# Top-32 attention and a routed MoE on one core: counts compared on GpSimd, and mask and maximum of 16 early tiles applied by TensorE products

## The chip, the cores and the metric

The kernel runs as one program on one core of one Trainium2 chip. A core has five engines that run their own instruction streams in order and meet at semaphores: TensorE (PE, with its weight loads shown as PEld), VectorE (DVE), ScalarE (ACT), GpSimd (POOL) and SyncE (SP, which only issues transfers here). The metric is the device time of the whole program in microseconds, as a median over runs.

## The reference

```python
scores = scale * np.matmul(q, k.transpose(0, 1, 3, 2))      # 8 batches, 8 heads, 576 x 576, head_dim 64
kth = np.partition(scores, -32, axis=-1)[..., -32:-31]
scores = np.where(scores >= kth, scores, -1000000000.0)
attn = np.exp(scores - np.max(scores, axis=-1, keepdims=True))
attn = attn / (np.sum(attn, axis=-1, keepdims=True) + 1e-09)
x = (attn @ v) laid out as 4608 tokens x 512
logits = x @ w_gate + modality_bias[modality_id]            # 8 experts
e_idx = np.argmax(logits, axis=1);  gate_w = softmax(logits) at e_idx
for e in range(8):                                          # every token goes to one expert
    out[e_idx == e] = gate_w[...] * (np.maximum(x[e_idx == e] @ w1[e], 0.0) @ w2[e])
```

## The kernel before

The scores are worked on in 288 tiles of 128 rows by 576 columns; a pair of heads is nine tiles, four pairs are one batch. One loop (L1123) has one pass per tile and works on tiles at different depths of a pipeline: in pass i TensorE computes the scores of tile i+2, VectorE takes the maxima of tile i in six pieces (L396) and merges those of tile i-1 (L407 to L409), ScalarE counts by a Sign with an accumulator how many scores lie above the 24th largest value (L428, tile i-3), GpSimd multiplies scores and signs into `y` (L434, tile i-4), VectorE takes the next eight values out of `y` (L438, tile i-5), and for every third tile it turns the counts of three tiles into the 32nd largest value `kth` (L445 to L447, `pick`): `eq` compares a table of numbers with the counts, `jk` multiplies it with the candidates, a sum leaves the threshold. At the end of pass i VectorE masks tile i-7. The transposes of tile i-9 follow on TensorE (L492), their evacuation on ScalarE (L500), and the products with V for roles 3, 7 and 8 of the nine (L520).

There are two ways to mask. For the tiles from 48 on, and for every third one before, ScalarE takes the exponential of the scores minus the row maximum (L452), and VectorE's `keep` (L458) multiplies it with the mask and sums the row. For the other tiles below 48 ("early", L1012), VectorE's `hide` (L465) writes a penalty of zero or minus 2^100, GpSimd adds it to the scores (L471, `ex<-Ssb,hT`), and ScalarE takes the exponential with the row sum (L477).

The order on VectorE inside a pass is written by a small planner (`arrange`, L949) from a table of durations; the other engines get the instructions as the code emits them. On GpSimd a pass is: the addition L471 for tile i-8, or for a tile masked by `keep` a one-element copy (`gate`, L481) that waits for `keep`; then `y` (L434), in every ninth pass the filling of the block-diagonal queries (L346), then the bound for the count (L421, `n`) and for every third tile the negated maxima (L415, `sm`).

The first batch has to be routed to its experts before the MoE products can start; until then TensorE runs six products with ones in each pass (`keep_warm`, L973), which nobody reads. From then on the MoE work is dealt out to the passes by a budget of TensorE cost per pass. What is left of it runs after the last tile. MoE weights lie in `w1b` and `w2b`, its gathered rows in `xgT` and its hidden layer in `hT`.

Of the kernel before, what the change touches and what calls it, by code (L numbers as in the profile page):

```python
# [35 lines left out]
QL = 2  # L36
KW = 10
FILL = 0
KP = 2
# [17 lines left out]
QO = 0  # L57
# [20 lines left out]
def kernel(  # L78
# [357 lines left out]
    def find(i):  # L436
        t = T[i]
        V.max(t["mg"][:, i % 3, 24:32], t["y"])  # L438

    def pick(i):  # L440

        t = T[i]
        eq, v = (wk.tile([128, 3, 9], FT, name=nm, bufs=1) for nm in ("eq", "jk"))
        n = t["n"][:, 0, :]
        return [lambda: V.tensor_tensor(eq, i9s, n[:, :, None].to_broadcast([128, 3, 9]), op=OP.is_equal),  # L445
                lambda: V.tensor_tensor(v, eq, t["mg"][:, :, 23:32], op=OP.mult),
                lambda: V.tensor_reduce(kth[:, i - 2:i + 1], v, axis=AX.X, op=OP.add)]  # L447
# [19 lines left out]
    def hidden(i):  # L467
# [1022 lines left out]
```

## Time and profile before

| | |
|---|---|
| median of 3 runs | 1193.73 us (1190.71 to 1193.77) |
| the profiled execution's own time | 1191.36 us |
| span of its profile | 1189.7 us |
| busy: PE, DVE, ACT, POOL | 1150.4, 1089.2, 981.5, 670.6 us |
| chain that ended last, by engine | PE 64%, DVE 23%, ACT 6%, issue 2%, DMA 2%, POOL 1% |

The time of the run has 1.7 us around the span. The busy time of an engine counts from the start of a record to its end, and records of neighbours overlap by some tens of nanoseconds on every engine, so what an instruction takes out of a stream is read from its start to the start of the next. The slices of the page show VectorE, TensorE and ScalarE nearly full from the second slice to the 34th (about 30 to 1000 us), and TensorE with VectorE at half from there on, where only MoE work is left.

### The profile page before, as it was taken

How to read it: one execution, taken by the hardware profiler on the slowest of the kernel's cores; microseconds unless marked ns; L12 is line 12 of the kernel's file. 1: busy time of each engine (PE TensorE's matmuls, PEld its weight loads, DVE VectorE, ACT ScalarE, POOL GpSimd, SP SyncE). 2: the span in 40 equal slices, each digit the busy share in tenths (PEclk: the TensorE clock that was granted, in tenths of full speed). 3: DMA queues.
4: the chain of work that ended last, by engine and by line, in shares of the span. 5: the costliest groups of instructions: out<-in, count | busy, mean ns of one | idle time of the engine just before them, and what ended most of it. 6: DMA issues, size and time to landing. Idle time of an engine off the chain costs nothing.

```text
span 1189.7 us, 28032 instructions
## 1 busy us (share of the span) xinstructions
PE 1150.4 (97%) x7902; PEld 904.1 (76%) x7902; DVE 1089.2 (92%) x5474; ACT 981.5 (83%) x2015; POOL 670.6 (56%) x1256
## 2 busy tenths in 40 slices
PE   8889979999999999999999999999999999999998
PEld 6667768777777868777686877778687777589987
DVE  7999999999999999999999899999999999476762
ACT  5999979998889979998999899989999887355653
POOL 6888875555656565566566566557655665221111
PEclk9999999999999999999999999999999999999999
DMA  5663357653677368654785448664765554287750
GB/s 125 161 183 90 89 164 221 191 151 87 169 221 199 86 178 241 170 151 129 199 244 156 129 134 242 168 163 133 204 185 134 173 145 148 71 288 250 245 191 22
DMA packets 204323, 197.09 MB, mean 166 GB/s; under 512 B 104413, under 2 KB 151533, under 8 KB 204160
## 3 DMA queue, kind: packets, MB, share of 16 engines
q1 hardware_dynamic: 196880, 175.92, 53.4%
q0 software_dynamic: 6080, 19.00, 4.4%
q8 instruction: 66, 1.08, 0.4%
q14 instruction: 97, 0.79, 0.2%
q10 hardware_dynamic: 1200, 0.30, 0.1%
HBM read 118.63 MB, written 24.23 MB: 120 GB/s over the span
## 4 chain that ended last, share of the span: by engine, by line
PE 64%; DVE 23%; ACT 6%; issue 2%; DMA 2%; POOL 1%; SPq 0%; POOLq 0%; ACTq 0%; DVEq 0%
PE E L798 11%; PE E L811 11%; PE X L520 10%; PE S L384 8%; PE T L492 7%; DVE cand L396 6%; PE X L1085 5%; PE X L1069 4%; DVE mg L438 4%; DVE P L458 4%; PE E L1069 1%; PE X L318 1%; ACT K L428 1%; ACT Ssb L389 1%; DVE cand L407 1%
## 5 line engine op out<-in xcount | busy, mean ns | idle before, releaser
L396 DVE MAX8 cand<-Ssb 128x8 f32<-128x96 f32 x1728 | 389.5, 245 | 2.1 <-ACT Ssb L389 2.1
L434 POOL TENSOR_TENSOR y<-Ssb,K 128x576 f32<-128x576 f32 x288 | 368.2, 1279 | 8.9 <-ACT K L428 8.6
L428 ACT ACTIVATE K<-Ssb,n 128x576 bf16<-128x576 f32 x288 | 230.0, 799 | 9.2 <-POOL y L434 9.0
L384 PE MATMUL S<-ks,qs 128*128 128x288 f32 x992 | 222.7, 346 | 9.9 <-ACT Ssb L389 6.5
L389 ACT ACTIVATE Ssb<-S 128x576 f32<-128x576 f32 x284 | 187.9, 662 | 53.5 <-PE S L384 32.4
L438 DVE MAX8 mg<-y 128x8 f32<-128x576 f32 x288 | 213.4, 741 | 3.9 <-POOL y L434 3.9
L798 PE MATMUL E<-xgT,w1b 128*128 128x256 f32 x832 | 201.2, 384 | 3.5 <-ACT hT L802 1.6
L452 ACT ACTIVATE ex<-Ssb,sm 128x576 f32<-128x576 f32 x256 | 202.9, 793 | 0.0
L500 ACT ACTIVATE PT<-T 128x640 f32<-128x640 f32 (+1 forms) x288 | 193.6, 672 | 6.7 <-PE T L492 6.6
L811 PE MATMUL E<-w2b,hT 128*128 128x512 f32 x416 | 195.8, 597 | 0.5 <-ACT hT L802 0.2
L384 PEld LDWEIGHTS S<-ks,qs 128*128 128x128 f32 x992 | 152.9, 190 | 56.8 <-issue 26.0
L458 DVE SCALAR_TENSOR_TENSOR P<-Ssb,kth,ex 128x576 f32<-128x576 f32 x230 | 191.3, 832 | 3.0 <-ACT ex L452 1.7
L492 PE MATMUL T<-idf,P 128*128 128x128 f32 x1152 | 169.6, 274 | 6.3 <-ACT P L477 5.3
L798 PEld LDWEIGHTS E<-xgT,w1b 128*128 128x128 f32 x832 | 150.8, 190 | 30.0 <-ACT hT L802 6.6
L481 POOL TENSOR_SCALAR spare<-P 1x1 f32<-1x1 f32 x230 | 41.9, 182 | 211.7 <-DVE mg L407 175.0
L492 PEld LDWEIGHTS T<-idf,P 128*128 128x128 f32 x1152 | 137.6, 141 | 12.5 <-ACT P L477 8.8
L520 PE MATMUL X<-PT,vm 128*64 128x256 f32 (+1 forms) x1536 | 145.2, 331 | 1.0 <-ACT xgT L757 0.5
L520 PEld LDWEIGHTS X<-PT,vm 128*64 128x64 f32 x1536 | 87.7, 137 | 45.3 <-issue 10.7
L421 POOL TENSOR_SCALAR n<-mg 128x1 f32<-128x1 f32 x288 | 67.5, 234 | 96.4 <-DVE mg L409 78.9
L811 PEld LDWEIGHTS E<-w2b,hT 128*128 128x128 f32 x416 | 72.6, 190 | 59.6 <-issue 54.7
L428 ACT ACTIVATION_READ_ACCUMULATOR K<-Ssb,n 128x1 f32 x288 | 64.0, 222 | 0.0
L1091 POOL DMA_INDIRECT out_dram<-ot,tk x12 | 12.3, 1026 | 91.0 <-ACT ot L1090 91.0
(223 smaller groups left out, 2146.5 us busy)
## 6 DMA issues: line engine op xcount, KB each, us to landing
w1b<-in_moe_w_dram SPq DMA_DIRECT2D x76, 512.0 KB
w2b<-in_moe_w_dram SPq DMA_DIRECT2D x76, 512.0 KB
ks<-st SPq DMA_DIRECT2D x62, 288.0 KB
ks<-st SPq DMA_DIRECT2D x62, 256.0 KB
qs<-st SPq DMA_DIRECT2D x124, 128.0 KB
xg<-xs SPq DMA_DIRECT2D x19, 516.0 KB
vm<-in_v_dram SPq DMA_DIRECT2D x32, 256.0 KB
km<-in_k_dram SPq DMA_DIRECT2D x63, 128.0 KB
```

The source lines that it names most:

```text
L384: PE.matmul(ps[:, hf, :288], l, m, start=(n == 0), stop=(n == len(terms) - 1))
L389: A.activation(sb.rearrange("p (a b) -> p a b", a=2), T[i]["ps"], AF.Copy, scale=0.125)
L396: return [lambda s=s: V.max(c[:, s * 8:s * 8 + 8], T[i]["S"][:, bnd[s]:bnd[s + 1]]) for s in range(NSUB)]
L428: A.activation(t["K"], t["S"], AF.Sign, scale=2.0 ** -24 - 1.0, bias=t["n"][:, 1, i % 3:i % 3 + 1], accum_out=t["n"][:, 0, i % 3:i % 3 + 1])
L434: G.tensor_tensor(t["y"], t["S"], t["K"], op=OP.mult)
L438: V.max(t["mg"][:, i % 3, 24:32], t["y"])
L452: A.activation(t["ex"], t["S"], AF.Exp, bias=t["s"][:, i % 3:i % 3 + 1])
L458: V.scalar_tensor_tensor(t["P"], t["S"], kth[:, i:i + 1], t["ex"], op0=OP.is_ge, op1=OP.mult, accum_out=dn)
L492: PE.transpose(T[i]["pt"][:, x, :], (Pm if c == 4 else Pb[c % 2])[:, h * 512 + x * 128:h * 512 + x * 128 + 128], idf)
L520: PE.matmul(o.rearrange("p (a b) -> p a b", a=2) if j < 8 else o, l, r, start=(c == 0), stop=(c == 4))
L798: PE.matmul(ps[:, f % 2], w1b[:, c, f * 128:(f + 1) * 128], xgT[:, c, :], start=(c == 0), stop=(c == KC - 1))
L811: PE.matmul(o["py"], hT[:, f, t * 128:(t + 1) * 128], w2b[:, f, :], start=(f == 0), stop=(f == FC - 1))
```

## The change

1. The comparison of table and counts (`eq`) leaves VectorE's `pick` and becomes one GpSimd instruction per tile (`which_count`, 128x9), right behind `y`.
2. All tiles below 36 are early now. Tiles with role 0 to 3 among them (four in each of the first four pairs, 16 in all) are "wide": their scores are evacuated into memory that later holds MoE weights (`swide`), VectorE writes a mask of one and zero (`hide_wide`), GpSimd makes a diagonal of the negated row maximum times 2^80 (`top_wide`, 128x128, a ring of three buffers), and TensorE adds to the transposes the product of mask and diagonal and a product that adds the maximum (`trans_wide`). ScalarE's evacuation of the transposes takes the exponential. The addition on GpSimd (L471) and the exponential L477 fall away for these tiles.
3. The row sums of the wide tiles come from TensorE: products with ones over the transposed tiles, a copy, two small products and another copy (`sums_wide`, one set per pair).
4. `keep_warm` is left out in the pass in which a pair's sums are queued and in the four after it (`quiet`).
5. A third check beside the two on the thresholds, on the row maxima, leads to the slow path that recomputes everything.

```diff
-FILL = 0
+WIDE = 36
+BIG = float(2.0 ** 80)
...
+    idw = const.tile([128, 128], BF, name="idw")
+    V.tensor_scalar(idw, idf, BIG * (1.0 + 2.0 ** -7), None, op0=OP.mult)
+    tops = const.tile([128, WIDE], FT, name="tops")
...
+    wide = lambda i: main[0] and i < WIDE and role(i) < 4
...
+    def which_count(i):
+
+        t = T[i]
+        x = i % 3
+        t["eq"] = T[i - 1]["eq"] if x else wk.tile([128, 3, 9], FT, name="eq", bufs=2)
+        G.tensor_scalar(t["eq"][:, x, :], i9s[:, x, :], t["n"][:, 0, x:x + 1], 1.0, op0=OP.is_equal, op1=OP.mult)
+
     def pick(i):

         t = T[i]
-        eq, v = (wk.tile([128, 3, 9], FT, name=nm, bufs=1) for nm in ("eq", "jk"))
-        n = t["n"][:, 0, :]
-        return [lambda: V.tensor_tensor(eq, i9s, n[:, :, None].to_broadcast([128, 3, 9]), op=OP.is_equal),
-                lambda: V.tensor_tensor(v, eq, t["mg"][:, :, 23:32], op=OP.mult),
+        eq, v = t["eq"], wk.tile([128, 3, 9], FT, name="jk", bufs=1)
+        return [lambda: V.tensor_tensor(v, eq, t["mg"][:, :, 23:32], op=OP.mult),
                 lambda: V.tensor_reduce(kth[:, i - 2:i + 1], v, axis=AX.X, op=OP.add)]
...
+    def hide_wide(i):
+
+        _, b, h = wide_of(i)
+        V.tensor_scalar(hwide[b][:, h * (S + 128):h * (S + 128) + S], T[i]["S"], kth[:, i:i + 1], 1.0,
+                        op0=OP.is_lt, op1=OP.mult)
+
+    def top_wide(i):
+
+        t = T[i]
+        t["dg"] = wk.tile([128, 128], BF, name="dg", bufs=3)
+        G.tensor_scalar(t["dg"], idw, t["s"][:, i % 3:i % 3 + 1], 1.0, op0=OP.mult, op1=OP.mult)
+
+    def trans_wide(i):
+
+        n, b, h = wide_of(i)
+        hb = hwide[b]
+        T[i]["pt"] = pt = psT.tile([128, 5, 128], FT, name="T")
+        for x in range(4 + h):
+            a = h * 512 + x * 128
+            PE.matmul(pt[:, x, :], swide[n][:, a:a + 128], idf, start=(x % 4 == 0), stop=False,
+                      is_transpose=True, skip_group_check=True)
+            for o, u in [(x * 128, i)] if not h else [(512, i - 1), (640, i)] if x == 0 else [(640 + x * 128, i)]:
+                PE.matmul(pt[:, x, :], hb[:, o:o + 128], T[u]["dg"], start=False, stop=False, skip_group_check=True)
+        dg = lambda u, n: T[u]["dg"][:, None, :].to_broadcast([128, n, 128])
+        for a, b, o, u in [(0, 4, 64, i)] if not h else [(0, 1, 128, i - 1), (0, 1, 0, i), (1, 4, 64, i), (4, 5, 64, i)]:
+            PE.matmul(pt[:, a:b, :], tiny[:, o:o + 128], dg(u, b - a), start=False, stop=True, skip_group_check=True)
+
+    def sums_wide(p):
+
+        st = {}
+
+        def part(c0, c1):
...
+            for c in range(c0, c1):
+                for h in range(2):
+                    PE.matmul(st["po"][h * 64:h * 64 + 64, :256].rearrange("p (a b) -> p a b", a=2),
+                              sel[:, 0 if c < 4 else 1 + h, :], PT[:, 0:2, c + 5 * h if c < 4 else 4, :],
+                              start=(c == 0), stop=(c == 4), skip_group_check=True)
...
+        return [(1.5, lambda: part(0, 3)), (1.0, lambda: part(3, 5)), (0.2, rows)]
...
-        A.activation(o, T[i]["pt"][:, :n], AF.Copy)
+        A.activation(o, T[i]["pt"][:, :n], AF.Exp if wide(i) else AF.Copy)
...
-    early = lambda u: u < EARLY and u % 3 != 2
+    early = lambda u: u < WIDE or u < EARLY and u % 3 != 2
...
-            hidden(i - 1 - LR)
+            (top_wide if wide(i - 1 - LR) else hidden)(i - 1 - LR)
...
-        if ok(u) and early(u):
+        if ok(u) and early(u) and not wide(u):
             masked(u, dn_of(u))
...
+            if role(u) == 3 and wide(u):
+                avs.extend(sums_wide(u // 9))
+                quiet[0] = i + 4
-        if not seen[0] and FILL <= i < NT:
+        if not seen[0] and quiet[0] < i < NT:
             keep_warm(NW)
...
-            end.append(Op("keep", lambda: hide(u) if early(u) else keep(u, dn_of(u)), got, *cut_))
+            end.append(Op("keep", lambda: hide_wide(u) if wide(u) else hide(u) if early(u) else keep(u, dn_of(u)), got, *cut_))
...
             pool_y(i - LY)
+            which_count(i - LY)
```

The two streams that the change reorders most are GpSimd's and VectorE's; the rows below are of pass 22 and its neighbours (the third pair of heads), with the program's names and their buffer numbers. First GpSimd before, from the `gate` of the pass that fills the queries (`qbd1`) to the next pass's additions:

```order
L481 TENSOR_SCALAR spare_170<-P0_119 1x1
L434 TENSOR_TENSOR y_1461<-Ssb_1077,K_1369 128x576
L346 TENSOR_SCALAR qbd1_116<-st_1187 64x2x64 x2
L421 TENSOR_SCALAR n_1465<-mg_1434 128x1
L415 TENSOR_SCALAR sm_1467<-mg_1270 128x3
L471 TENSOR_TENSOR ex_1469<-Ssb_902,hT_140 128x576
L434 TENSOR_TENSOR y_1528<-Ssb_1137,K_1420 128x576
```

The same passes of GpSimd in the changed kernel (L508 is the addition that was L471, L466 is `y`, L477 the moved comparison, L366 the filling, L453 `n`, L447 the maxima):

```order
L508 TENSOR_TENSOR ex_1437<-Ssb_875,hT_140 128x576
L466 TENSOR_TENSOR y_1499<-Ssb_1106,K_1397 128x576
L477 TENSOR_SCALAR eq_1501<-i9s_102,n_1312 128x9
L366 TENSOR_SCALAR qbd1_116<-st_1205 64x2x64 x2
L453 TENSOR_SCALAR n_1505<-mg_1475 128x1
L447 TENSOR_SCALAR tops_170<-mg_1288 128x3
L508 TENSOR_TENSOR ex_1508<-Ssb_937,hT_140 128x576
L466 TENSOR_TENSOR y_1558<-w1b_128,K_1460 128x576
```

The pass with the filling began with the one-element copy and begins with an addition now, and a comparison stands behind each `y`. Third, GpSimd at the wide tiles of the pair before, in the changed kernel alone, with the semaphores that each instruction waits for:

```order
L520 TENSOR_SCALAR dg_792<-idw_168,tops_170 128x128 [waits Pool_49]
L466 TENSOR_TENSOR y_851<-Ssb_515,K_734 128x576 [waits Activation_49]
L477 TENSOR_SCALAR eq_787<-i9s_102,n_628 128x9
L453 TENSOR_SCALAR n_789<-mg_765 128x1 [waits DVE_49]
L520 TENSOR_SCALAR dg_856<-idw_168,tops_170 128x128 [waits PE_49,Pool_49]
L466 TENSOR_TENSOR y_908<-Ssb_550,K_815 128x576 [waits Activation_49]
```

The fourth diagonal of a pair takes the buffer of the first, and so waits for TensorE. Last, VectorE in the pass that picks, before:

```order
L396 MAX cand_1437<-Ssb_1319 128x8
L445 TENSOR_TENSOR eq_1438<-i9s_102,n_1116 128x27
L409 MAX mg_1434<-cand3_1436 128x8
L396 MAX cand_1437<-Ssb_1319 128x8
L446 TENSOR_TENSOR jk_1439<-eq_1438,mg_1091 128x27
L396 MAX cand_1437<-Ssb_1319 128x8
L447 TENSOR_REDUCE kth_127<-jk_1439 128x3
```

and in the changed kernel (L427 was L396, L440 was L409, L483 and L484 are the rest of `pick`):

```order
L427 MAX cand_1478<-w1b_128 128x8
L483 TENSOR_TENSOR jk_1479<-eq_1310,mg_1118 128x27
L440 MAX mg_1475<-cand3_1477 128x8
L427 MAX cand_1478<-w1b_128 128x8
L484 TENSOR_REDUCE kth_127<-jk_1479 128x3
L427 MAX cand_1478<-w1b_128 128x8 x2
L502 TENSOR_SCALAR hT_140<-Ssb_937,kth_127 128x576
```

The product `jk` stands where the comparison stood, one piece and the last merge earlier than before.

## Rows read from the trace of the kernel before

**Rows 1.** Busy us (instructions) per stretch: PE, PEld, DVE, ACT, POOL; PEclk, DMA, GB/s.
```profile
90.00:120.00 30.00, 27.10 (x228) 20.74 (x228) 30.00 (x162) 28.80 (x66) 24.92 (x36) 1.00 0.39 89
...
200.00:1000.00 800.00, 792.94 (x5340) 610.02 (x5340) 785.73 (x4194) 715.37 (x1483) 479.42 (x943) 1.00 0.61 169
```

**Rows 2.** Chain of waits from 190 to 1000 us, shares by line.
```profile
by line: PE E L798 15.4%; PE E L811 15.2%; PE X L520 12.6%; PE S L384 10.8%; PE T L492 9.1%; DVE cand L396 5.7%; DVE P L458 4.2%; DVE mg L438 3.7%; PE X L318 1.7%; issue 1.4%; DVE cand L407 1.2%; DVE cand L408 1.2%; ACT K L428 1.1%; PE X L2
```

**Rows 3.** Timeline of VectorE: start us, us, engine line op out<-in [idle before].
```profile
90.59 0.20 DVE L409 MAX8 mg<-cand 128x8 f32<-128x48 f32 x1
...
91.38 0.50 DVE L465 TENSOR_SCALAR hT<-Ssb,kth 128x576 bf16<-128x576 f32 x1
91.79 0.20 DVE L407 MAX8 mg<-cand 128x8 f32<-128x48 f32 x1
...
94.11 0.70 DVE L465 TENSOR_SCALAR hT<-Ssb,kth 128x576 bf16<-128x576 f32 x1
94.72 0.20 DVE L407 MAX8 mg<-cand 128x8 f32<-128x48 f32 x1
...
97.04 1.07 DVE L458 SCALAR_TENSOR_TENSOR P<-Ssb,kth,ex 128x576 f32<-128x576 f32 x1
...
98.03 0.20 DVE L407 MAX8 mg<-cand 128x8 f32<-128x48 f32 x1
...
99.76 0.23 DVE L445 TENSOR_TENSOR eq<-i9s,n 128x27 f32<-128x27 f32 x1
...
100.71 0.50 DVE L465 TENSOR_SCALAR hT<-Ssb,kth 128x576 bf16<-128x576 f32 x1
...
118.29 0.16 DVE L445 TENSOR_TENSOR eq<-i9s,n 128x27 f32<-128x27 f32 x1
118.38 0.20 DVE L409 MAX8 mg<-cand 128x8 f32<-128x48 f32 x1
```

**Rows 4.** Timeline of GpSimd beside the same tiles.
```profile
91.96 1.28 POOL L471 TENSOR_TENSOR ex<-Ssb,hT 128x576 f32<-128x576 f32 x1 [0.60 <-DVE hT L465]
93.19 1.29 POOL L434 TENSOR_TENSOR y<-Ssb,K 128x576 f32<-128x576 f32 x1
94.57 0.28 POOL L421 TENSOR_SCALAR n<-mg 128x1 f32<-128x1 f32 x1
94.95 1.29 POOL L471 TENSOR_TENSOR ex<-Ssb,hT 128x576 f32<-128x576 f32 x1
...
99.67 0.67 POOL L346 TENSOR_SCALAR qbd<-st 64x128 fp32r<-64x128 f32 x2
...
100.67 0.20 POOL L415 TENSOR_SCALAR sm<-mg 128x3 f32<-128x3 f32 x1
```

**Rows 5.** Timeline of all engines around 300 us, the rows of GpSimd and VectorE.
```profile
299.88 1.27 POOL L434 TENSOR_TENSOR y<-Ssb,K 128x576 f32<-128x576 f32 x1
...
300.10 1.10 DVE L445 TENSOR_TENSOR eq<-i9s,n 128x27 f32<-128x27 f32 x1
```

**Rows 6.** Timeline of TensorE beside the tiles of rows 3.
```profile
90.19 1.95 PE L520 MATMUL X<-PT,vm 128*64 128x256 f32 x16
...
94.28 0.71 PE L492 MATMUL T<-idf,P 128*128 128x128 f32 x5
...
95.06 0.83 PE L973 MATMUL E<-onesb 128*128 128x256 bf16 x6
95.64 0.78 PE L384 MATMUL S<-ks,qs 128*128 128x288 f32 x4
```

**Rows 7.** Timeline of GpSimd at the start.
```profile
6.58 0.67 POOL L346 TENSOR_SCALAR qbd<-ks 64x128 fp32r<-64x128 f32 x2 [0.81 <-DVE ks L293]
```

**Rows 8.** Timeline of VectorE where the MoE work starts.
```profile
172.29 0.76 DVE L438 MAX8 mg<-y 128x8 f32<-128x576 f32 x1 [2.05 <-POOL y L434]
```

**Rows 9.** Busy time and granted clock of two short stretches, columns as in rows 1.
```profile
32.00:34.00 2.00, 0.99 (x8) 0.90 (x9) 2.00 (x8) 2.00 (x6) 1.84 (x4) 0.90 0.58 171
34.00:36.00 2.00, 2.00 (x11) 1.98 (x11) 2.00 (x15) 1.03 (x3) 1.17 (x3) 0.50 0.05 14
```

More of the change, by code (lines that the diff above doesn't have):

```diff
@@ L70 @@
 EARLY = 48
+WIDE = 36
+BIG = float(2.0 ** 80)
+MAX_TOP = 64.0
 EPS = 1e-9
@@ L230 @@
     mbt = const.tile([128, 2, E], FT, name="mbt")
+    flat = lambda t: t.rearrange("p a b -> p (a b)")
+    swide = [flat(t)[:, n * 2 * S:(n + 1) * 2 * S] for t, n in ((w1b, 0), (w1b, 1), (w1b, 2), (w2b, 0))]
+    sel = flat(w2b)[:, 2 * S:2 * S + 192].rearrange("p (x d) -> p x d", x=3)
+    stage = flat(w2b)[:, 2 * S + 192:2 * S + 448]
+    hwide = [flat(t)[:, o:o + 640].bitcast(BF) for t, o in ((xgT, 0), (hT, 1024))]
+    G.memset(sel[:, 0:1, :], 1.0)
+    G.memset(sel[:, 1:3, :], 0.0)
+    for x in range(2):
+        G.memset(sel[x * 64:x * 64 + 64, 1 + x, :], 1.0)
+        G.memset(hwide[x][:, S:S + 128], 0.0)
+    idw = const.tile([128, 128], BF, name="idw")
+    V.tensor_scalar(idw, idf, BIG * (1.0 + 2.0 ** -7), None, op0=OP.mult)
+    tops = const.tile([128, WIDE], FT, name="tops")
+    tiny = flat(w2b)[:, 2 * S + 448:2 * S + 576].bitcast(BF)
+    G.memset(tiny[:, 64:192], 1.0 / BIG)
+    G.memset(tiny[:, 0:64], 0.0)
+    G.memset(tiny[:, 192:256], 0.0)
+    main = [True]
     zr = const.tile([128, XW], FT, name="zr")
@@ L355, with wide_of @@
     role = lambda i: (i - 1) % 9
+    wide = lambda i: main[0] and i < WIDE and role(i) < 4
+    def wide_of(i):
+        c, h = divmod(role(i), 2)
+        return (i // 9 * 2 + c) % 4, c % 2, h
     def unstacked(j):
@@ L387, in sevac @@
     def sevac(i):
-        T[i]["S"] = sb = wk.tile([128, S], FT, name="Ssb", bufs=LR + 1 + QL - QO)
+        if wide(i):
+            n, _, h = wide_of(i)
+            sb = swide[n][:, h * S:h * S + S]
+        else:
+            sb = wk.tile([128, S], FT, name="Ssb", bufs=LR + 1 + QL - QO)
+        T[i]["S"] = sb
         A.activation(sb.rearrange("p (a b) -> p a b", a=2), T[i]["ps"], AF.Copy, scale=0.125)
@@ L411, in small @@
     def small(i0):
-        s = wk.tile([128, 3], FT, name="sm", bufs=6)
+        on = main[0] and i0 < WIDE
+        s = tops[:, i0:i0 + 3] if main[0] and i0 < WIDE else wk.tile([128, 3], FT, name="sm", bufs=6)
         for x in range(3):
             T[i0 + x]["s"] = s
-        G.tensor_scalar(s, T[i0]["mg"][:, :, 0], -1.0, 1.0, op0=OP.mult, op1=OP.mult)
+        G.tensor_scalar(s, T[i0]["mg"][:, :, 0], -1.0, 0.0 if on else 1.0, op0=OP.mult, op1=OP.min if on else OP.mult)
     def below(i):
@@ new lines, in sums_wide, with rows @@
+    def sums_wide(p):
+        st = {}
+        def part(c0, c1):
+            if c0 == 0:
+                st["po"] = psE.tile([128, 260], FT, name="E")
+            for c in range(c0, c1):
[3 more added lines that the diff above has]
+                              start=(c == 0), stop=(c == 4), skip_group_check=True)
+            if c1 == 5:
+                xev.append(lambda: A.activation(stage, st["po"][:, :256], AF.Copy))
+        def rows():
+            for c in range(2):
+                PE.matmul(st["po"][:, 256 + 2 * c:258 + 2 * c], stage[:, c * 128:c * 128 + 128], idf[:, 0:128:64],
+                          start=(c == 0), stop=(c == 1), skip_group_check=True)
+            xev.append(lambda: A.activation(den[p // HP % 2][:, p % HP, 0:4], st["po"][:, 256:260], AF.Copy))
+        return [(1.5, lambda: part(0, 3)), (1.0, lambda: part(3, 5)), (0.2, rows)]
@@ L489, in trans @@
         c, h = divmod(role(i), 2)
+        if wide(i):
+            trans_wide(i)
+            return
         T[i]["pt"] = psT.tile([128, 5, 128], FT, name="T")
@@ L975 @@
     keep_warm(KW)
-    bd_ = const.tile([128, 4], FT, name="bad")
+    bd_ = const.tile([128, 6], FT, name="bad")
     badi = const.tile([1, 1], I32, name="badi")
@@ L983, in bounds @@
         V.tensor_scalar(bt, kth, KTH_MAX, 0.0, op0=OP.is_ge, op1=OP.add, accum_out=bd_[:, 1:2])
+        V.tensor_scalar(bt[:, :WIDE], tops, -MAX_TOP, 0.0, op0=OP.is_le, op1=OP.add, accum_out=bd_[:, 2:3])
     def beyond():
-        bb = bd_.bitcast(BF)[:, 4:6]
-        V.tensor_scalar(bb, bd_[:, 0:2], 0.0, None, op0=OP.is_gt)
-        pbad = psX.tile([128, 2], FT, name="X")
+        bb = bd_.bitcast(BF)[:, 8:11]
+        V.tensor_scalar(bb, bd_[:, 0:3], 0.0, None, op0=OP.is_gt)
+        pbad = psX.tile([128, 3], FT, name="X")
         PE.matmul(pbad, onesb, bb, start=True, stop=True)
@@ L1016 @@
     turn = [0]
+    quiet = [-1]
     def acc(shape):
@@ L1271 @@
             if (i - LT) % 3 == 2:
-                e_, v_, s_ = pick(i - LT)
-                e_ = Op("pick", e_)
-                v_ = Op("pick", v_, e_, found)
+                v_, s_ = pick(i - LT)
+                v_ = Op("pick", v_, found)
                 got = Op("pick", s_, v_)
-                ops += [e_, v_, got]
+                ops += [v_, got]
         ops += run("late", lo)
@@ L1379 @@
     slot(SURE)
-    bad = nc.values_load(badi[:, :], min_val=0, max_val=256)
-    more = nc.values_load(morei[:, :], min_val=0, max_val=N + 256)
+    bad = nc.values_load(badi[:, :], min_val=0, max_val=384)
+    more = nc.values_load(morei[:, :], min_val=0, max_val=N + 384)
     slot(None)
@@ L1407, in slow @@
     def slow():
+        main[0] = False
         Pb[:] = [wk.tile([128, 2 * S], FT, name=f"P{i}", bufs=1) for i in range(2)]
```

## The prediction

> **What bounds the kernel now.** I read the page's slices first, then busy time by stretch, the chain of waits, and the timelines of single engines. In the first batch VectorE has no gap: 30.00 us busy in 30, with ScalarE at 28.80, TensorE at 27.10 (products that nobody reads included) and GpSimd at 24.92. From 200 to 1000 us TensorE is the full one (792.9 of 800), VectorE has 785.7, GpSimd only 479.4 [rows 1]. The chain of waits there runs mostly over TensorE's lines; VectorE's pieces and merges (L396, L407, L408), `find` (L438) and `keep` (L458) hold 5.7 + 3.7 + 4.2 + 1.2 + 1.2 = 16.0% of it [rows 2]. So there are two stages. Early, a tile takes as long as VectorE needs, and since the MoE starts in a fixed pass, a microsecond lost or won there should reach the end. Later a microsecond off VectorE is worth roughly its share of the chain.
>
> An early triple is a hidden tile of 94.72 - 91.79 = 2.93 us, a `keep` tile of 98.03 - 94.72 = 3.31, and a picking tile. Nine tiles take 118.38 - 90.59 = 27.79 us [rows 3], so the picking tile has 9.26 - 6.24 = 3.02. VectorE and GpSimd hinder each other: `hide` takes .41 (91.38 to 91.79) when GpSimd is idle, .61 (94.11 to 94.72) when `y` is running, and the first addition starts .17 after `hide` gives way [rows 3, 4]. At 300 us the comparison `eq`, .16 us of work, lasted 1.10 and ended with the `y` beside it (301.20 against 301.15) [rows 5].
>
> **The early tiles, by parts.** I lay out nine tiles anew, four wide and five hidden.
>
> VectorE's work between a tile's start and its `hide` is 94.11 - 91.79 = 2.32 us. In a picking tile it is 100.71 - 98.03 = 2.68; without `eq`, which takes 118.38 - 118.29 = .09 there, 2.59 [rows 3].
>
> Wide: GpSimd has no addition, `y` comes earlier, and `hide_wide` should get its .41. I take 2.93 for the first, 2.32 + .41 = 2.73 for two, 2.59 + .41 = 3.00 for the one that picks: 11.4 us. Four average tiles of before had 4 x 3.09 = 12.4, so 1.0 is won.
>
> Hidden: now five stand in a row. GpSimd's chain there was addition, `y`, bound: 94.95 - 91.96 = 2.99 from addition to addition [rows 4], already longer than VectorE's 2.93, and relieved in every third tile by `keep`, which has no addition (`gate` .18). That relief is gone, and each round gets a comparison of 128x9. No row shows one on GpSimd; its nearest rows are the negated maxima 128x3 at .20 and the bound 128x1 at .28 [rows 4], so I take .2 and a round of 3.2 us. In two of the five a pick falls. There `jk` takes the slot of `eq`, 99.76 - 98.03 = 1.73 after the tile's start [rows 3], but the addition has moved `y` to stand over that slot: it starts 93.19 - 91.79 = 1.40 after the start, and lets go at about 2.52 (it ends at 94.48, VectorE's `hide` beside it had its way .17 before). `jk` has two inputs as `eq` had, so I let it wait 2.52 - 1.73 = .79: 3.00 + .79 = 3.79. The five are 2.73 for the first, which follows a wide tile, 2 x 3.2 and 2 x 3.79: 16.7, and with .2 for the filling (.67 us at 99.67 [rows 4]), which now stands in a tile with an addition, 16.9.
>
> Sum: 28.3 against 27.79, .5 more per nine tiles. The bounds are wide. If nothing of the collisions bites, the five are 3 x 2.73 + 2 x 3.00 = 14.2 and the nine 25.6, that is -2.2. If the filling costs its whole .67 and the comparison .28, the nine have some .9 more.
>
> A wait is added. The ring of diagonals has three buffers, so a pair's fourth waits on GpSimd for the transposes of the wide tiles that used the first; `y`, the comparison and the bound are queued behind it, and `find` on VectorE waits for `y`. Before, the transposes of a tile ended at 94.28 + .71 = 94.99, 3.2 us after the start of VectorE's tile [rows 6]; with some ten products more, about 1.2 us at the price below, 4.4. The diagonal stands a pass later, so it starts 4.4 - 2.73 = 1.7 into that pass, and `y` ends .2 + .1 + 1.29 after, at 3.3, where `find` wants it at 2.73 or, after a pick, 3.00: .3 to .6 late. With cheaper products it is 0, with products of twice that price and a later start on TensorE about 1. I take .3. So .8 per nine tiles, and for the three and a half such groups up to tile 36 **+2.8 us** (bounds -8 and +6).
>
> TensorE gets, per pair, 20 mask products of 128 columns, five small ones, and the sums. A 256-column step of `onesb` is .11 (95.06 to 95.64 for six, .58, counts as .10) [rows 6]; the mask products are between half of that and the whole, 1.1 to 2.2, the small ones as much as 1.1 together, and the 20 passes of the sums 2.2 by the same price. That is 4.4 to 5.5, less five `keep_warm` of .58, 2.9: +1.5 to +2.6 per 28 us, beside 30 - 27.10 = 2.90 idle in 30 [rows 1]. I take 0; VectorE's full row is the cover. If the cover fails, it is the fall of the clock, a rival below. ScalarE loses 16 exponentials and gains the same count of evacuations with one: 0.
>
> The nine extra fills at the start, about .1 each by L415's .20, lie beside .81 of GpSimd's idle time [rows 7]: 0 (to +.3).
>
> **From tile 36 on.** Without `eq` VectorE has .09 less in each of some 80 later picks: 7.2 us if it were the only bound, and by 16.0% [rows 2] **-1.2** (0 to -7). GpSimd's comparison costs .2 in 240 passes, 48 us, and fits in the 320 us that it is idle [rows 1]. `jk` inherits the stalls of `eq` [rows 5], since it is the same kind of instruction in nearly the same place. Where the MoE starts, GpSimd is behind: `find` waited 2.05 us for `y` [rows 8]. The comparison that now stands behind each `y` lengthens that queue by .2 a pass in about five passes, and half of it counts: **+.5** (0 to +1.4).
>
> The Trainium skill (Perfetto Trace Analysis, "Optimizing Scalar/DVE Operations") says that GpSimd and VectorE share a read port of the SBUF, so that moving operations between those two might not help. By that rule the -1.2 would be nothing, and the sum +3.3. The stretched `eq` [rows 5] agrees with a shared port; no row here shows a comparison that has been moved.
>
> **Sum.** 2.8 - 1.2 + .5 = +2.1 us. The profiled execution took 1191.36 (span 1189.7 and 1.7 around it); with the sum 1193.5. The median of the runs shown is 2.4 above that execution, so I forecast 1193.73 + 2.1 = **1195.8 us**.
>
> **Rivals.**
>
> B, faster: the collisions do not bite in the five hidden tiles. `arrange` puts VectorE's instructions by its table, and GpSimd's chain may settle so that `jk` falls between addition and `y`. Then up to 2.2 is won per nine tiles, 8 in all, and the later picks keep their share: with half to all of it, 1193.73 - 4 - 1.2 to 1193.73 - 8 - 2. I take 1187 (1182 to 1190). For it: `hide` at .41 when GpSimd is idle [rows 3], and the wide tiles. Against: the 2.99 of GpSimd's round [rows 4], which does not shrink.
>
> C, slower: TensorE becomes the bound in the five passes without its unread products. After a stretch with TensorE .99 busy in 2.00, the granted clock was .50 from 34 to 36 us, the lower of its two levels (1.2 GHz) [rows 9]. Should that return in every quiet stretch, the products with V, 92.86 - 90.19 = 2.7 us [rows 6] at full clock, take 5.4 or more, the next transposes come as much later, and with them the fourth diagonal, `y` and `find`: some 2.5 per pair, four times, less what VectorE's slack absorbs: +5 to +10, 1199 to 1204, centre 1202. It decides from the point where a quiet pass of TensorE exceeds VectorE's 3 us. For it: the start of the run. Against: the mask products and sums keep TensorE busy in just these passes.
>
> **How the numbers follow.** About .3% (3.6 us: 1190.1 and 1197.3) is what a measurement can tell from no change. My forecast A has .42, its own range 1192 to 1200: .34 within, .08 slower. B has .36: .34 faster, .02 within. C has .22, all slower. Together faster .34, same .36, slower .30. The range goes from 1184, which leaves the far end of B out, to 1204, the end of C.
>
> **What the profile after would show.** For A: VectorE's tiles at about 2.7 in the wide part and 3.2 and 3.8 in the five others; `jk` about 1 us long in those that pick; GpSimd's fourth diagonal waiting for TensorE; comparisons of .2; the granted clock full after 40 us; the stretch from 200 to 1000 us shorter by a microsecond or so. B shows as `jk` at .16 and tiles of at most 3 us throughout. C shows as a granted clock of .50 in the passes behind each pair's sums, with VectorE idle before `find`. I am wrong if the comparison on GpSimd is far from .2, or if the later stretch moves by more than 3 us either way.

## The result, and the profile after

The changed kernel took 1208.80 us as the median of five runs (1206.60 to 1210.95), against 1193.73 before: slower, by a ratio of 1.014 (95% interval 1.012 to 1.0161). The medians lie 15.1 us apart; the ratio, taken over all runs of both (before: 1190.13 to 1193.80), stands for 16.7. The prediction was 1195.8 with a range to 1204. The profiled execution has a span of 1207.1 us, 17.4 more than before. One run of the experiment e10 below is left out of its ratio: it took 1915 us at a mean granted clock of .56, and why stays open.

Where it went is read from the starts of VectorE's last merge of each tile (L409 before, L440 after). The 46th comes at 146.2 us before and at 158.3 after, 12.1 later; the 73rd is 12.4 later, the 253rd 16.0. So 12 us are lost in the first 45 tiles and some 4 to 5 after the 73rd. The busy time per stretch of the changed kernel answers to [rows 1] (same columns):

```profile
90.00:120.00 30.00, 28.55 (x227) 21.85 (x227) 27.54 (x137) 23.98 (x55) 25.23 (x39) 0.89 0.47 115
200.00:1000.00 800.00, 790.19 (x5351) 609.18 (x5348) 777.24 (x4101) 712.25 (x1481) 570.33 (x1168) 1.00 0.62 168
```

VectorE, without a gap before, now idles 2.5 us in 30, and the granted clock has a mean of .89. GpSimd is 91 us busier in the later stretch. Two groups of the page say what the comparison takes (busy us, mean ns of one | idle before, releaser), and that `find` now waits 18.6 us for `y` in all:

```profile
L470 DVE MAX8 mg<-y 128x8 f32<-128x576 f32 x288 | 212.6, 738 | 18.6 <-POOL y L466 18.6
...
L477 POOL TENSOR_SCALAR eq<-i9s,n 128x9 f32<-128x9 f32 x288 | 105.9, 368 | 1.9
```

The comparison is 368 ns on average, not 200. GpSimd's timeline, while VectorE takes the maxima of the third pair, shows both early losses, the wait of the second pair's fourth diagonal and the length of the round (from one addition to the next):

```profile
68.89 0.19 POOL L453 TENSOR_SCALAR n<-mg 128x1 f32<-128x1 f32 x1
72.49 0.37 POOL L520 TENSOR_SCALAR dg<-idw,tops 128x128 bf16<-128x128 bf16 x1 [3.41 <-PE T L535]
72.82 1.28 POOL L466 TENSOR_TENSOR y<-Ssb,K 128x576 f32<-128x576 f32 x1
...
80.26 1.51 POOL L466 TENSOR_TENSOR y<-w1b,K 128x576 f32<-128x576 f32 x1
...
82.44 1.29 POOL L508 TENSOR_TENSOR ex<-Ssb,hT 128x576 f32<-128x576 f32 x1
83.69 1.28 POOL L466 TENSOR_TENSOR y<-w1b,K 128x576 f32<-128x576 f32 x1
85.08 0.42 POOL L477 TENSOR_SCALAR eq<-i9s,n 128x9 f32<-128x9 f32 x1
85.58 0.19 POOL L453 TENSOR_SCALAR n<-mg 128x1 f32<-128x1 f32 x1
85.85 1.28 POOL L508 TENSOR_TENSOR ex<-Ssb,hT 128x576 f32<-128x576 f32 x1
```

The round from addition to addition is 85.85 - 82.44 = 3.41 us where it was 2.99 [rows 4], with no gap: GpSimd sets the pace of these tiles. VectorE beside it:

```profile
74.14 0.76 DVE L470 MAX8 mg<-y 128x8 f32<-128x576 f32 x1 [1.59 <-POOL y L466]
...
75.76 0.34 DVE L483 TENSOR_TENSOR jk<-eq,mg 128x27 f32<-128x27 f32 x1
...
81.80 0.76 DVE L470 MAX8 mg<-y 128x8 f32<-128x576 f32 x1 [1.06 <-POOL y L466]
...
84.01 1.28 DVE L502 TENSOR_SCALAR hT<-Ssb,kth 128x576 bf16<-128x576 f32 x1
```

`find` waits 1.59 behind the late diagonal, and that tile takes 4.69 us (merge to merge) instead of 3.46. It waits 1.06 more at 81.80, in the tile behind the filling of the queries. `hide` at 84.01 lasts 1.28 where it took .61 [rows 3]: it gets through only when the `y` beside it is done (83.69 + 1.28 = 84.97), while `jk` is hardly stretched. The diagonal waited for TensorE, whose granted clock had fallen; two stretches (columns of rows 1) and two rows of its timeline:

```profile
60.00:62.00 2.00, 0.88 (x6) 0.65 (x6) 2.00 (x6) 1.63 (x6) 1.83 (x5) 0.83 0.88 228
62.00:64.00 2.00, 1.78 (x9) 1.65 (x10) 2.00 (x13) 1.71 (x6) 1.92 (x3) 0.50 1.01 382
```

```profile
66.15 2.90 PE L609 MATMUL X<-PT,vm 128*64 128x256 f32 x16
...
72.10 0.49 PE L535 MATMUL T<-dg,w2b 128*128 128x128 bf16 x4
```

After a stretch in which TensorE was .88 busy in 2.00 the clock is .50, the lower of its two levels; the products with V take 2.90 us instead of 1.95 [rows 6], and the last products with the first diagonal, which release its buffer, run from 72.10 to about 72.5. So rival C, the fall of the clock with its late diagonal, happened as described, and yet the experiments give it the smaller part of the loss.

### The profile page after: what moved, and what is told of

Its sections match the earlier page's. It is cut to its first block, busy times and chain, and to the rows that moved or that the text cites. A ratio compares the mean times of both kernels' runs of the same rounds, so it can differ in the third digit from the quotient of the medians.

```text
span 1207.1 us, 28374 instructions
## 1 busy us (share of the span) xinstructions
PE 1165.5 (97%) x7998; PEld 913.4 (76%) x7998; DVE 1088.3 (90%) x5369; ACT 974.0 (81%) x2003; POOL 781.6 (65%) x1553
## 4 chain that ended last, share of the span: by engine, by line
PE 54%; DVE 30%; POOL 6%; ACT 5%; issue 3%; DMA 1%; SPq 0%; POOLq 0%; ACTq 0%; DVEq 0%
PE E L900 9%; PE X L609 8%; PE E L887 8%; DVE cand L427 8%; PE S L410 6%; DVE mg L470 5%; PE T L581 5%; DVE P L495 5%; PE X L1176 5%; PE X L1160 4%; POOL y L466 3%; DVE cand L438 2%; DVE cand L439 2%; POOL ex L508 1%; PE E L1160 1%
## 5 line engine op out<-in xcount | busy, mean ns | idle before, releaser
L427 DVE MAX8 cand<-Ssb 128x8 f32<-128x96 f32 x1632 | 357.3, 241 | 1.1 <-ACT Ssb L420 1.1
L466 POOL TENSOR_TENSOR y<-Ssb,K 128x576 f32<-128x576 f32 x272 | 347.7, 1278 | 14.2 <-ACT K L460 12.8
L460 ACT ACTIVATE K<-Ssb,n 128x576 bf16<-128x576 f32 x272 | 216.0, 794 | 19.0 <-POOL y L466 18.9
L470 DVE MAX8 mg<-y 128x8 f32<-128x576 f32 x288 | 212.6, 738 | 18.6 <-POOL y L466 18.6
L420 ACT ACTIVATE Ssb<-S 128x576 f32<-128x576 f32 x270 | 177.6, 658 | 47.7 <-PE S L410 32.9
L489 ACT ACTIVATE ex<-Ssb,sm 128x576 f32<-128x576 f32 x244 | 193.0, 791 | 0.0
L495 DVE SCALAR_TENSOR_TENSOR P<-Ssb,kth,ex 128x576 f32<-128x576 f32 x218 | 179.8, 825 | 5.0 <-ACT ex L489 2.5
L581 PE MATMUL T<-idf,P 128*128 128x128 f32 x1080 | 157.9, 273 | 1.6 <-ACT P L563 0.7
L581 PEld LDWEIGHTS T<-idf,P 128*128 128x128 f32 x1080 | 128.9, 140 | 5.9 <-ACT P L563 2.5
L609 PEld LDWEIGHTS X<-PT,vm 128*64 128x64 f32 x1536 | 88.9, 139 | 50.1 <-issue 12.9
L477 POOL TENSOR_SCALAR eq<-i9s,n 128x9 f32<-128x9 f32 x288 | 105.9, 368 | 1.9
L453 POOL TENSOR_SCALAR n<-mg 128x1 f32<-128x1 f32 x288 | 73.5, 255 | 43.5 <-DVE mg L440 17.7
```

Of the source, the lines that this page charges most:

```text
L427: return [lambda s=s: V.max(c[:, s * 8:s * 8 + 8], T[i]["S"][:, bnd[s]:bnd[s + 1]]) for s in range(NSUB)]
L460: A.activation(t["K"], t["S"], AF.Sign, scale=2.0 ** -24 - 1.0, bias=t["n"][:, 1, i % 3:i % 3 + 1], accum_out=t["n"][:, 0, i % 3:i % 3 + 1])
L466: G.tensor_tensor(t["y"], t["S"], t["K"], op=OP.mult)
L489: A.activation(t["ex"], t["S"], AF.Exp, bias=t["s"][:, i % 3:i % 3 + 1])
L495: V.scalar_tensor_tensor(t["P"], t["S"], kth[:, i:i + 1], t["ex"], op0=OP.is_ge, op1=OP.mult, accum_out=dn)
L609: PE.matmul(o.rearrange("p (a b) -> p a b", a=2) if j < 8 else o, l, r, start=(c == 0), stop=(c == 4))
```

## The experiments

Each kernel was timed against the kernel before on its own chip. The last columns are one profiled execution: how much later than before VectorE's 46th, 73rd and 253rd last merge start, and the span ends. Runs of one kernel differ by some microseconds, so these columns are rough: e12 has 2.8 there, and 1.5 by its median.

| run | ratio (95% interval) | 46th | 73rd | 253rd | end |
|---|---|---|---|---|---|
| changed kernel | 1.0140 (1.0120 to 1.0161) | 12.1 | 12.4 | 16.0 | 17.4 |
| e1 comparison alone | 1.0111 (1.0093 to 1.0129) | 8.2 | 8.9 | 12.5 | 15.0 |
| e2 wide tiles alone | 1.0026 (1.0014 to 1.0037) | 2.7 | 3.8 | 3.4 | 3.4 |
| e3 changed, products kept | 1.0108 (1.0092 to 1.0124) | 6.9 | 7.0 | 11.1 | 13.4 |
| e4 changed, ring of four | 1.0093 (1.0077 to 1.0110) | 7.3 | 7.4 | 11.6 | 12.7 |
| e5 unread comparison added | 1.0120 (1.0101 to 1.0138) | 8.4 | 10.5 | 16.0 | 16.5 |
| e6 one per three tiles | 1.0008 (0.9995 to 1.0020) | 0.1 | -0.7 | 2.6 | 3.4 |
| e7 wide alone, ring of four | 1.0016 (1.0004 to 1.0027) | 1.7 | 1.9 | 1.4 | 1.4 |
| e8 the same, `keep` back | 0.9971 (0.9959 to 0.9983) | -2.9 | -2.9 | -3.5 | -3.5 |
| e9 the same, products kept | 1.0015 (1.0004 to 1.0027) | 0.9 | 3.1 | 3.5 | 3.5 |
| e10 comparison last | 1.0078 (1.0059 to 1.0097) | 5.9 | 6.7 | 11.5 | 13.0 |
| e11 e8 and late comparison | 1.0000 (0.9989 to 1.0012) | -2.4 | -3.0 | 0.0 | 1.1 |
| e12 unread memset added | 1.0005 (0.9992 to 1.0018) | 0.4 | 0.5 | 2.8 | 2.8 |

### e1: the comparison alone

```diff
 # in the kernel before
+            which_count(i - LY)
-        return [lambda: V.tensor_tensor(eq, i9s, ...is_equal),
-                lambda: V.tensor_tensor(v, eq, ...
+        return [lambda: V.tensor_tensor(v, eq, ...
```

> The kernel before with one edit: the comparison is on GpSimd, behind each y; no wide tiles. My theory after the result: the comparison costs .34 to .43 us of GpSimd in each pass (not .2), y comes later by that, and find waits for y; so it costs time in both stages. From 72 passes on the changed kernel lost some 4 us, and I expect these here too: +4 to +7 us, find's waits for y grown from 3.9 us toward 18. Rival (my prediction's step): GpSimd has 40% idle time, the comparison hides there, and VectorE's saved instruction wins about 1.2 us: -3 to +1.

Measured: 1205.38 against 1191.81, +13.6 us; nearly the whole loss, and twice what I expected. The early tiles, by GpSimd's rows and then VectorE's:

```profile
99.43 1.29 POOL L476 TENSOR_TENSOR ex<-Ssb,hT 128x576 f32<-128x576 f32 x1
100.67 1.29 POOL L434 TENSOR_TENSOR y<-Ssb,K 128x576 f32<-128x576 f32 x1
102.06 0.72 POOL L445 TENSOR_SCALAR eq<-i9s,n 128x9 f32<-128x9 f32 x1
```

```profile
101.11 1.47 DVE L463 SCALAR_TENSOR_TENSOR P<-Ssb,kth,ex 128x576 f32<-128x576 f32 x1
```

In the kernel before, `keep` at 97.04 took 1.07 [rows 3] beside the `y` of this row, which stands right behind the addition at 94.95 [rows 4]:

```profile
96.20 1.29 POOL L434 TENSOR_TENSOR y<-Ssb,K 128x576 f32<-128x576 f32 x1
```

It had begun .84 us before `keep`. In e1 two comparisons have moved `y` later, so that it begins .44 us before `keep`, and `keep` stands behind it for .4 us more. Nothing shows as a wait; it is inside the duration. Over the early tiles (14 to 146 us before, 14 to 154 in e1) the mean of `keep` goes from 1.05 to 1.45, that of `hide` from .60 to .68, that of `jk` from .17 to .35. A part of the later loss shows in the passes in which GpSimd sends rows to the experts (`xs<-x,dest`, an indirect transfer). Before, around 814 us, GpSimd first, then VectorE:

```profile
814.50 1.28 POOL L611 DMA_INDIRECT xs<-x,dest  x1 [0.17 <-issue]
...
816.38 1.27 POOL L434 TENSOR_TENSOR y<-Ssb,K 128x576 f32<-128x576 f32 x1
```

```profile
816.61 1.09 DVE L445 TENSOR_TENSOR eq<-i9s,n 128x27 f32<-128x27 f32 x1
```

and in e1, the same pass:

```profile
828.31 0.97 POOL L616 DMA_INDIRECT xs<-x,dest  x1 [0.17 <-issue]
...
829.91 1.27 POOL L434 TENSOR_TENSOR y<-Ssb,K 128x576 f32<-128x576 f32 x1
831.18 0.84 POOL L445 TENSOR_SCALAR eq<-i9s,n 128x9 f32<-128x9 f32 x1
```

```profile
827.84 0.76 DVE L438 MAX8 mg<-y 128x8 f32<-128x576 f32 x1 [1.45 <-POOL y L434]
...
830.31 1.50 DVE L463 SCALAR_TENSOR_TENSOR P<-Ssb,kth,ex 128x576 f32<-128x576 f32 x1
```

With a send, `y` and the small pieces GpSimd was full for the whole pass; the comparison goes on top, `find` waits 1.45, and the stall that `eq` had is passed on to `keep`. In groups of twelve tiles from the 73rd merge on, the six with such sends take 4.2 us more than before in all. That is not the whole: four without one (from the 73rd, 145th, 181st and 217th) take 3.5 more, and in the last three of them `jk` falls on `y` where neither it nor `eq` did before. One case stands behind a transfer of results, again on GpSimd:

```profile
651.39 1.65 POOL L831 DMA_INDIRECT out_dram<-ot,stok  x1 [0.17 <-issue]
...
653.63 1.27 POOL L434 TENSOR_TENSOR y<-Ssb,K 128x576 f32<-128x576 f32 x1
...
653.75 1.20 DVE L451 TENSOR_TENSOR jk<-eq,mg 128x27 f32<-128x27 f32 x1
```

In the other seven groups VectorE's saved instruction does show, 3.1 us in all: the twelve tiles from the 97th (and the 205th, the 241st), with four picks, are .45 to .5 us shorter than before.

### e2, e7, e8, e9: the wide tiles alone

```diff
 # e2, in the changed kernel
-            which_count(i - LY)
+        (eq back in pick, on VectorE)
 # e7, in e2
-        t["dg"] = wk.tile([128, 128], BF, name="dg", bufs=3)
+        t["dg"] = wk.tile([128, 128], BF, name="dg", bufs=4)
 # e8, in e7
-    early = lambda u: u < WIDE or u < EARLY and u % 3 != 2
+    early = lambda u: wide(u) or u < EARLY and u % 3 != 2
 # e9, in e8
-                quiet[0] = i + 4
+        (while the sums' tile is held, the unread products add to its columns 264 to 511)
```

> The changed kernel with the comparison back on VectorE; wide tiles, quiet passes and the rest as changed. My theory: the loss of 15 us has two parts that add, the comparison (5 to 9 us) and the fall of TensorE's clock with the wait of the fourth diagonal (6 to 8 us). This should come back to +6 to +9 us over before, with the clock still at half in the passes behind each pair's sums and the wait of 3.4 us before the fourth diagonal still there. Rival: the fall of the clock explains nearly all; then this stays at +13 or more.

> The wide tiles alone (comparison on VectorE), with four buffers for the diagonals. The wide tiles with three measured +3.1 us. Theory: of these the fourth diagonal's wait makes about 1 to 2, the rest are the two stalls of eq per pair of 1.0 us beside y in the five hidden tiles: +1 to +2 here, with eq still 1.0 us long twice in a pair. Rival: the wait is covered by TensorE's being behind, and the time stays at +3.

> As the run before, and of the five other tiles of a pair every third is masked by keep again, as in the kernel before. Theory: the additions no longer stand in five passes in a row, GpSimd gets its relief back, eq is no longer beside y, and the four wide tiles of 2.7 to 3.0 us instead of 3.1 give 1 us per pair: -2 to -5. Rival: what the wide tiles win is lost again by TensorE at half clock in the passes without unread products: 0 to +3.

> The run with the wide tiles and keep in every third of the other tiles (3.5 us faster than before), now with the unread products in every pass of the first batch; in the passes that hold the sums' accumulator they add to columns 264 to 511 of its tile, which nobody reads. It prices the fall of TensorE's clock behind each pair's sums. Theory: VectorE sets the pace there and the fall is hidden, since the ring of four took the fourth diagonal off it: the granted clock is full after 40 us and the time stays within 1 us of that run (-2.5 to -4.5 against before). Rival: the low clock still costs time; then another 1.5 to 4 us are won (-5 to -8).

Measured: e2 +3.1 us, less than I expected, and with e1's 13.6 it makes 16.7, the ratio of the whole change (.014 of 1192). That they add is not a rule: with a ring of four the comparison costs some 9 to 10 on top of the wide tiles (e4 against e7), not 13.6. e7, +1.9, gains 1.2 on e2, though their intervals meet. e8, -3.5, is faster than before. What stood in its way is `eq` in the five hidden tiles, as a row of e2 shows; in e8, where every third of these tiles goes back to `keep`, `eq` takes .16:

```profile
72.05 1.00 DVE L477 TENSOR_TENSOR eq<-i9s,n 128x27 f32<-128x27 f32 x1
```

```profile
70.96 0.16 DVE L477 TENSOR_TENSOR eq<-i9s,n 128x27 f32<-128x27 f32 x1
```

e9 went the other way from both theories: keeping the unread products costs 5.2 us (1.0015 against .9971), though the clock is full in both kernels here. Two stretches of e8, then of e9:

```profile
60.00:80.00 20.00, 20.00 (x192) 16.06 (x191) 20.00 (x108) 17.67 (x41) 16.34 (x24) 1.00 0.65 182
80.00:100.00 20.00, 18.43 (x176) 15.34 (x176) 20.00 (x111) 17.32 (x40) 15.12 (x26) 1.00 0.51 131
```

```profile
60.00:80.00 20.00, 19.98 (x193) 16.44 (x192) 20.00 (x103) 17.59 (x42) 14.95 (x22) 1.00 0.60 166
80.00:100.00 20.00, 19.98 (x190) 16.31 (x189) 20.00 (x111) 16.92 (x39) 13.84 (x22) 1.00 0.42 120
```

In e8 the clock does not fall in these stretches though the products are left out (it did at 30 to 36 us): with tiles of 2.7 to 3.4 us TensorE has more to do in the same time. With them one tile of each pair takes 3.8 to 3.9 us instead of 2.93. TensorE comes to the next scores and transposes later, so ScalarE's count `K` ends later, `y` waits for it, and `jk`, .17 in e8, stands behind `y`, as two rows of e9 show; where the first batch is routed, VectorE then waits for TensorE, which it does not in e8:

```profile
71.28 1.28 POOL L467 TENSOR_TENSOR y<-Ssb,K 128x576 f32<-128x576 f32 x1 [1.46 <-ACT K L461]
```

```profile
71.57 1.03 DVE L479 TENSOR_TENSOR jk<-eq,mg 128x27 f32<-128x27 f32 x1
...
154.51 0.40 DVE L670 TENSOR_TENSOR lt<-X,rd 128x128 f32<-128x128 f32 x1 [2.14 <-PE X L662]
```

So the quiet passes are needed. That the clock fell in the changed kernel because its tiles were stretched is an inference from this. e1 and e5 bear it out: they have no wide tiles and all of their unread products, but longer tiles, and their clock falls as well, where it was 1.00 before. Two stretches of e1 (the two from 56 to 60 us have TensorE .83 and .93 busy of 2.00 each, against 1.28 and 1.59 before):

```profile
58.00:60.00 2.00, 0.93 (x5) 0.70 (x6) 2.00 (x8) 2.00 (x5) 1.84 (x4) 1.00 0.94 243
60.00:62.00 2.00, 2.00 (x11) 1.61 (x12) 2.00 (x14) 1.37 (x4) 2.00 (x2) 0.55 1.02 378
```

### e3, e4: the clock and the ring

```diff
 # e3, in the changed kernel
-                quiet[0] = i + 4
+            if held[0] is not None:
+                PE.matmul(held[0][:, 264:512]..., onesb, ..., start=True, stop=True)
 # e4, in the changed kernel
-        t["dg"] = wk.tile([128, 128], BF, name="dg", bufs=3)
+        t["dg"] = wk.tile([128, 128], BF, name="dg", bufs=4)
```

> The changed kernel with the six unread products in every pass of the first batch (in the passes that hold the sums' accumulator they write into columns 264 to 511 of its tile). My theory: the clock stays at full after 40 us, the products with V take 1.95 and not 2.9 us, the fourth diagonal waits under 1 us instead of 3.4, and 5 to 8 us of the 15 come back: +7 to +10 over before. Rival: TensorE's added work alone makes it late; then the unread products put it further behind, and the time is the changed kernel's or more (+15 to +18).

> The changed kernel with four buffers for the diagonals instead of three, so that a pair's fourth no longer waits for the transposes of the same pair. My theory: GpSimd's wait of 3.4 us per pair goes, find's wait of 1.6 with it, while the clock still falls: 3 to 5 us come back (+10 to +12 over before). Rival: TensorE is behind anyway by the low clock, so that the next scores or the counts are late in its place and VectorE waits there: no more than 1 us comes back.

Measured: e3 +12.9, e4 +11.6: of 16.7 us 4 and 5 come back, in e3 less than I expected (its interval meets that of the changed kernel, e4's does not). In e3 the unread products spoil the row sums of the wide tiles, so its routing can differ and only its early tiles are read here. A stretch of e3 and one of e4, and e4's fourth diagonal, which waits for nothing:

```profile
60.00:80.00 20.00, 19.73 (x190) 16.11 (x189) 20.00 (x101) 17.03 (x40) 17.63 (x31) 1.00 0.56 157
```

```profile
80.00:100.00 20.00, 17.40 (x132) 12.95 (x132) 20.00 (x102) 14.58 (x34) 18.52 (x30) 0.83 0.40 112
```

```profile
68.13 0.69 POOL L520 TENSOR_SCALAR dg<-idw,tops 128x128 bf16<-128x128 bf16 x1
```

From 40 us to the end of the early tiles the clock is whole in e3; in e4 it still falls, at 34 to 38 and at 88 to 95 us. Both bring the 46th merge to about +7: they take away the same wait from its two sides. The low clock costs most of its time through the diagonal, but not all of it: the nine tiles from the 28th merge, behind a fall, take 29.8 us in e4, the nine before them, at full clock, 29.1, and the changed kernel's 31.1 and 31.3.

### e5, e6, e10, e11, e12: what of the comparison costs

```diff
 # e5, in the kernel before (eq stays on VectorE; nobody reads eqg)
+        G.tensor_scalar(t["eqg"][:, x, :], i9s[:, x, :], t["n"][:, 0, x:x + 1], 1.0, op0=OP.is_equal, op1=OP.mult)
 # e12, the same with
+        G.memset(t["eqg"][:, x, 0:1], 0.0)
 # e6, in e1
+        if x == 2:
+            G.tensor_tensor(t["eq"], i9s, n..., op=OP.subtract)
+        V.scalar_tensor_tensor(v, eq, 0.0, mg..., op0=OP.is_equal, op1=OP.mult)
 # e10, in e1: which_count(i - LY) behind small(i - 4), not behind pool_y
 # e11, in e8: the same place, for tiles from 48 on only
```

> The kernel before, its comparison left on VectorE, with a second one on GpSimd behind each y that nobody reads. It parts the two ways in which the moved comparison can have cost 13.6 us. Theory 1, the time on GpSimd: .33 to .72 us more in each pass behind y shift the bound, the next addition and the next y, and VectorE's hide, keep and picks run into a y that comes later; then the unread one costs as much, +12 to +16. Theory 2, the new dependence: jk and the threshold wait for GpSimd's result; then the unread one costs 0 to +4.

> The kernel before with one instruction on GpSimd for three tiles instead of three: the difference of table and counts (128x27), and jk on VectorE takes the comparison with zero and the product in one instruction. Theory 1: the cost goes with the time on GpSimd per pass; one instruction of .3 to .7 us in every third pass instead of each leaves a third, +3 to +6. Theory 2: the dependence costs; then +11 to +15 as with three.

> The kernel before with the comparison moved to GpSimd as in the first experiment (+13.6 us), but at the end of GpSimd's pass, behind the bound and the maxima, not behind y. From 240 us on GpSimd waits there for keep, some 1 us in most passes. Theory: the cost is a matter of the place; late nothing is behind it that anyone waits for, and the .1 us a pick that VectorE saves shows, so from pass 72 on -3 to 0 against before instead of +6; early the addition follows at once and some of the 8 us stay, +2 to +6. Together -1 to +5. Rival: the time of the comparison on GpSimd counts wherever it stands, +11 to +15.

> The wide tiles with a ring of four and keep in every third of the other tiles, and the comparison on GpSimd at the end of its pass, for the tiles from 48 on alone; before that it stays on VectorE. Theory: the early gain of 3.5 us stays and the later one adds 1 to 3: -4 to -6.5 against before. Rival: the comparison costs wherever it stands, and the gain is lost: 0 to +3.

> As the run with the unread comparison on GpSimd behind each y (+14.8 us), but the unread instruction is a memset of one column, of some .1 us (the trace has .09 for such) instead of .33 to .72. Theory: the duration on GpSimd is what costs, so a quarter to a third of it costs +2 to +5. Rival: the instruction as such, its issue and its place between y and the bound, costs; then +12 to +15.

Measured: e5 +14.8 (as theory 1 had it), e6 +1.0 and e12 +1.5 (by the ratio of 1.0005, +.6), both less than I expected, e10 +9.7 by the median of its five other runs, between theory and rival, e11 -.4, near the rival. GpSimd's groups of e5 and e12 from the table of all lines, and `keep` in e5:

```profile
L445 POOL TENSOR_SCALAR eqg<-i9s,n 128x9 f32<-128x9 f32 x288 | 107.8, 374 | 1.9
```

```profile
L445 POOL MEMSET eqg<- 128x1 f32 x288 | 26.3, 91 | 0.0
```

```profile
101.63 1.46 DVE L465 SCALAR_TENSOR_TENSOR P<-Ssb,kth,ex 128x576 f32<-128x576 f32 x1
```

An unread comparison costs as much as a read one, so the new dependence is not the cause; 91 ns in its place cost nothing that can be measured, so neither is the issue of one more instruction. It is the 370 ns, with one open end: the memset's row has no input, so e12 alone does not part the time from the reading. e6 reads, and is one instruction of 343 ns for three of 380. e6, a third of the time, and e12, a quarter, both cost within their intervals of nothing: the cost grows faster than the time. Probably `y` clears `keep` and the next pass up to some point; no run here places that point. My theory on the place fell with e10: of 13.6 us only some 4 come back (the intervals overlap), and late it is no better than e1 (5.7 us lost from the 73rd to the last merge, against 4.0). It moves more than the place, though: the comparison lasts 630 ns on average there, 380 in e1. In e11 the gain of e8 is lost between the 145th merge and the end. Two rows of VectorE from e11, in the same passes with a send as in e1:

```profile
814.88 0.76 DVE L470 MAX8 mg<-y 128x8 f32<-128x576 f32 x1 [1.19 <-POOL y L466]
...
816.81 1.42 DVE L486 TENSOR_TENSOR jk<-eq,mg 128x27 f32<-128x27 f32 x1 [0.23 <-POOL eq L477]
```

In neither place that was tried has a pass with a send room for the comparison. The difference of e1 and e5 would price what VectorE is spared, -1.2 us, but their intervals overlap.

## Why the prediction was wrong

- The step that failed is "GpSimd's comparison costs .2 in 240 passes, 48 us, and fits in the 320 us that it is idle". Both halves: it is .37, and idle time on average is no cover. In passes with a transfer on GpSimd there is none, and in some others the later `y` catches `jk`; the later stretch lost 4 to 6 us where -1.2 stood. Both signs of being wrong that the prediction names came: a comparison far from .2, and more than 3 us in this stretch.
- The same .2 was in the early sum, for the hidden tiles only. I priced one fate of the longer round, `jk` caught by `y`; in the early tiles of the changed kernel `jk` takes .17 to .51. What the runs show is that other instructions of VectorE that fall on `y` are caught: `keep` in e1 (1.47 for 1.07), `hide` in the changed kernel (1.28 for .61). The filling, at .2 in the sum, has a wait of 1.06 in `find` behind it. The comparison alone took 8.2 us from the early tiles, without a wide one.
- The layout of the wide tiles held where no comparison stands on GpSimd. With `eq` on VectorE nine tiles take 28.2 to 29.1 us (e2), against 28.3 forecast and .3 for the diagonal. The second pair's four wide tiles take 2.98, 2.81, 3.10 and 2.73, 11.6 against 11.4, and its five hidden ones 16.6 against 16.9. That the five agree is in part luck: two of them stall by some .85 (1.00 for .16) where .79 was taken, but it is `eq` that stalls, which the forecast had taken off VectorE.
- The fourth diagonal, .3 in the sum and about 1 at most, waited 3.1 to 3.4 us in three of four pairs and cost some 1.2 per pair (4.8 at the 46th merge, e4). The mechanism was named in rival C, but its price belongs to the forecast case too; C was then +5 to +10 in all, and e3 and e4 give it 4 to 5.
- That VectorE's saved `eq` is worth about .1 a pick was right where nothing falls on `y`; there it counts whole (.45 to .5 in four picks), not by the chain's 16%. Rival B, a win from the wide tiles, was right of another kernel: e8.
- The Trainium skill (Perfetto Trace Analysis, "Optimizing Scalar/DVE Operations") has the warning that fits: GpSimd and VectorE share a read port, so moving work between them might not help. I let it cancel the -1.2; the trace agrees with more than that, since e5 adds work on GpSimd alone and VectorE's `keep` grows from 1.07 to 1.46.

## What to carry to other kernels

Do not cover an instruction by an engine's idle share over a long stretch: look at the fullest kind of pass, here the ones in which GpSimd also has a transfer, and at what stands behind the instruction there. Where two engines hold each other up inside their instructions, a shift of one by .4 us shows as no wait at all; compare durations of the same line before and after. And before a rule is spread to all tiles, see whether the tile that is left out (here `keep` in every third) was what let the slower engine catch up.

## What the runs showed of the hardware

A comparison of 128x9 on GpSimd took .42 us in the changed kernel's row, .72 and .84 in e1 where VectorE's `keep` had begun beside `y`: GpSimd's small instruction behind `y` waits in its turn, and ends .2 us after `keep` in both. A memset of one column in the same place took .09. And the clock of TensorE did not fall in e8 in the quiet passes of the second and third pair, in which it fell in the changed kernel; TensorE was busy 18.4 us and more of each 20 there. In e1, with no quiet pass, it fell to a mean of .55 at 60 to 62 us, after TensorE was busy .83 and .93 in two stretches of 2.00.
